# Float32 attention jobs: scores of two heads as row tiles, high parts read from PSUM, moved priorities

## The chip, the cores and the metric

One core of a Trainium2 chip runs the kernel in one launch. The metric is the device time of that launch in microseconds. Names of engines: TensorE (PE in the profile, its weight loads PEld), VectorE (DVE), ScalarE (ACT), GpSimd (POOL); SP issues nearly all DMAs.

## The reference

```python
B, H, S, D = 4, 8, 768, 64
scores = (1 / np.sqrt(D)) * np.matmul(q, k.transpose(0, 1, 3, 2))
keep = (pos[None, :] < n_sink) | ((rel >= 0) & (rel < window))
...
attn = np.matmul(softmax_over_kept_keys, v)
x = attn.transpose(0, 2, 1, 3).reshape(B * S, H * D)
h = np.maximum(x @ moe_w_in, 0.0); y = h * h @ moe_w_out
h = y @ moe2_w_in; out = (h - np.tanh(h)) @ moe2_w_out
```

Four sequences of 768 positions and eight heads of 64 go through attention with 4 sink keys and a window of 128. The result, 3072 rows of 512, goes through two layers with 2048 inner columns: a squared relu, and h - tanh(h). Weights and results are finer than a single rounded product gives: the output must match a float32 (weights: wider) computation.

## The kernel before, in words

**Tiles and stages.** The 3072 rows are eight blocks of 384 (half a sequence each). Attention of a block is eight jobs, one per head (`job`, L294). A job has three query tiles of 128; each meets at most 260 keys and writes one score tile into a PSUM bank. The jobs of blocks 0 and 1 (j < 16, "plain", L452) multiply in float32; the later ones (`scores`, L324, `values`, L412) split q, k and v into a high and a low part of a faster type (float32r) and add products. The layers do the same: every weight half (16 x 2 of each layer) is loaded as 64-bit words (`w_load`, L552), turned into a high and a low part by five or six VectorE or ScalarE instructions (`w_split`, L558), and every product is three matmuls (`mm_a`, L591, line 600; `mm_b`, L605, lines 614 and 616). `step1` (L619) is one of 16 steps of the first layer for a block, `step2` (L651) one of the second for 512 rows.

**A plain job before the change.** q and k lie twice in a tile "raw", on both halves of the 128 partitions (`layout`, L1076), so that a matmul over 128 partitions gives twice the score; the scale of -0.0625 takes that back (L478, L487). For j > 1 each job loads its tile (L305) and its values (L306); the first two are loaded ahead in `prepare` (L832). There are four raw tiles and four value tiles. Then: three score matmuls (L471), for block 0 into two sets of "wide" banks that heads use in turn (`place`, L463), for block 1 into the bank S; a masked copy inside the bank (L475, L482); a minimum with the mask added, written to pcb (`least`, L398, line 403); the exponential (L489); sums, a reciprocal, the scaling (L501, L503); four transposes into the bank T (L512, L513); copies out of it (L271 on ScalarE, L273 on VectorE: the shared `copy`, L265); two triangular selects on POOL (L523, L526). After every second head, `plain_values` (L531) multiplies with the values of two heads, each on its own 64 columns of the array (L539, L544), into the bank O. The result of the pair is copied to px (L548), and `split` (L444) copies px to the high part xh and subtracts to get the low part xl (L449, in the shared `sub`, L276, line 281). xh and xl of all four pairs are the input of the block's 16 steps.

**What sets the order.** `plan` (L699) adds some 6,100 entries with a priority each (lower is earlier; due times worked out from rates per block), what they read and write, and a cost for each engine that could do them (the functions c_act to c_mm, L215 to L250). `Order.solve` (L127) goes through them as a list scheduler and picks for each entry its engine and place; the program is then emitted in that order (L821). Every engine's queue runs in order, SP's loads among them. `run` (L805) takes the tiles and zeroes the sink tiles psk (L814); `switch` (L785) lets tiles of one stage take the room of those of an earlier one.

Of the kernel before, what the change touches and what calls it, by code (L numbers as in the profile page):

```python
# [24 lines left out]
P = 128  # L25
# [34 lines left out]
SQ_S, SQ_B, SQ_D = _fit()  # L60

# [17 lines left out]
class Order:  # L79
# [46 lines left out]

    def solve(self):  # L127
        free = {e: self.AHEAD.get(e, 0.0) for op in self.ops for e in op.engs}
        avail, pend = {e: [] for e in free}, {e: [] for e in free}
# [113 lines left out]
def c_sel(n):  # L243
    return C(0.55 * n + 480, 0.55 * n + 530, True)

# [7 lines left out]
class Fast:  # L253
# [40 lines left out]
    def job(self, j, due):  # L294

        t = self.t
        blk, head = divmod(j, H)
        b, half = divmod(blk, 2)
        plain = j < PLAIN
        nk, nv, k2 = KW[half], NV[half] - 2 * (not plain), j % 2  # L300
        q, r = (j % 4, j % 4) if plain else (k2, j % 3)
        d = due[0]
        if j > 1:
            src, early = self.raw[half][b * H + head], 8 * plain
            self.load(d - 24 - early, [("rq", q), ("rk", q)], lambda: (t["raw", q][:, :QW[half]], src[:, :QW[half]]), P * QW[half] * 4)  # L305
            self.load(d - 23 - early, [("rv", r)], lambda: (t["rv", r][:, :nv * D], src[:, RW[half] - nv * D:]), P * nv * D * 4)  # L306

        def vals():
            return t["rv", r][:, :nv * D].rearrange("p (n d) -> p n d", d=D)
        if plain:  # L310
            self.plain(j, half, head, blk, q, due)
            return
        x = t["raw", q]
        self.copy(d - 16, [("rq", q)], [("qh", k2), ("ql", k2)], lambda: (t["qq", k2], x[:, :N1]), N1)
        self.sub(d - 15, [("rq", q)], [("ql", k2)], lambda: (t["qq", k2][64:], x[64:, :N1], t["qq", k2][64:]), N1)
        self.copy(d - 16, [("rk", q)], [("kh", k2)], lambda: (t["kh", k2][:, :nk], x[:, N1:N1 + nk]), nk)
        self.sub(d - 15, [("rk", q), ("kh", k2)], [("kl", k2)], lambda: (t["kl", k2][:, :nk], x[:, N1:N1 + nk], t["kh", k2][:, :nk]), nk)
# [134 lines left out]
    def plain(self, j, half, head, blk, q, due):  # L452
# [9 lines left out]

        def place(i):  # L463
            return bank["wide", m2, 0] if wide and i == 0 else bank["wide", m2, 1][:, i - 1, :] if wide else bank["S", 0]

        for i in range(3):
            sb = [("wide", m2, i)] if wide else [("S", 0)]
            col, n = self.keys(half, i)

            o.add({"T": c_mm(n, n, slow=1.85)}, due[i] - 14, [("rq", q), ("rk", q)], sb,  # L470
                  lambda e, i=i, col=N1 + col, n=n: nc.tensor.matmul(out=place(i)[:, :n], lhsT=t["raw", q][:, i * P:(i + 1) * P],  # L471
                                                                     rhs=t["raw", q][:, col:col + n], start=True, stop=True))
            if i >= i0 and not wide:
                o.add({"V": c_two(P, True)}, due[i] - 12, sb, sb,
                      lambda e, i=i: nc.vector.copy_predicated(out=place(i)[:, 132:260], mask=self.c["up"][:, 0, :], data=place(i)[:, :128]))  # L475
            if not wide:
                self.least(due[i] - 11, sb, [cbs[i], (*nm, i)], lambda i=i, n=n: place(i)[:, n - 132:n], lambda i=i: t[cb][:, i, :],
                           lambda i=i: t[nm][:, i:i + 1], half, i, -0.0625)  # L478
        if wide:
# [3 lines left out]
        for i in range(3):  # L483
            ks, n = cbs[i:i + 1], self.keys(half, i)[1]
            if wide:
                self.least(due[i] - 11, [("wide", m2, i)], [cbs[i], (*nm, i)], lambda i=i, n=n: place(i)[:, n - 132:n], lambda i=i: t[cb][:, i, :],
                           lambda i=i: t[nm][:, i:i + 1], half, i, -0.0625)  # L487
            o.add({"A": c_sum(132)}, due[i] - 10, ks + [(*nm, i)], ks + [(*ss, i)],
# [42 lines left out]
    def plain_values(self, half, head, blk, j, d):  # L531
        nc, o, t, bank = self.nc, self.o, self.t, self.bank
        ob, x, wins = ("O", 0), ("px", head // 2 % 2), self.windows(half)
        jobs = [(64 * k, (j + k) % 4) for k in range(2)]
# [12 lines left out]
        o.add({"T": C(t_mm, t_mm + 165.0)}, d - 4, [(n, k) for _, k in jobs for n in ("rv", "pps")] + [("ppp", k, i) for _, k in jobs for i in range(3)], [ob], pv)  # L547
        self.copy(d - 3, [ob], [x], lambda: (t[x], bank[ob][:, :N1]), N1, True)  # L548
        self.split(head, blk, d, x, [x])

# [148 lines left out]
    def plan(self):  # L699
# [32 lines left out]
        for q in range(4):  # L732
            if q == 2:
                self.switch(lambda k: k[0][0] == "p" and k[0] not in ("ph", "pt", "pts") or k in (("rq", 2), ("rq", 3), ("rk", 2), ("rk", 3), ("rv", 3)),
                            own, self.x_plain, self.attn)
            for n in range(8):
                self.step1(q % 2, n + 8 * (q // 2), PV[q] + n * PS[q], q // 2)
            if q > 1:
                attention(q)
# [21 lines left out]
        for t in range(NB2):  # L761
            for n in range(NM):
# [7 lines left out]
            ("xe", 1, (6, P), F32R), ("pt", 1, (12, P), F32R), ("pts", 2, (N1,), F32R), ("tmp", 1, (512,), F32), ("x", 1, (N1,), F32))  # L770
    PLAINS = (("raw", (2, 3), (QW[1],), F32), ("rv", (3,), (NV[1] * D,), F32), ("pcb", 4, (3, 132), F32), ("pnm", 4, (3,), F32), ("pss", 4, (3,), F32),
              ("prs", 4, (3,), F32), ("pxe", 2, (3, P), F32), ("ppp", 4, (6, P), F32), ("psk", 2, (96,), F32), ("pps", 4, (P,), F32), ("px", 2, (N1,), F32))
    AFTER = (("x2h", 2, (NE, N2), F32R), ("x2l", 2, (NE, N2), F32R))
# [31 lines left out]
    def run(self):  # L805
        tc, nc = self.tc, self.nc
        with ExitStack() as self.st:
# [5 lines left out]
            for i in range(2):  # L813
                nc.gpsimd.memset(self.t["psk", i], 0.0)  # L814
            pool = self.x_wide.enter_context(tc.tile_pool(name="wide", bufs=1, space=PSUM, reuse_waits="tile"))
            for i in range(2):
# [8 lines left out]
def prepare(tc, cp, ns_wd, f, raw):  # L825
# [6 lines left out]
    for j in range(2):  # L832
        (nc.sync if j else nc.scalar).dma_start(out=f.t["raw", j][:, :QW[0]], in_=raw[0][j, :, :QW[0]])
    for j in range(2):
# [241 lines left out]
def layout(q, k, v, n_sink, window, moe_w_in, moe_w_out, moe2_w_in, moe2_w_out):  # L1076
# [10 lines left out]
    for half, ks, vs_ in ((0, [sk, kb[0], sk, kb[1], sk, kb[2]], range(3)), (1, [kb[2], sk, kb[3], sk, kb[4], sk, kb[5]], range(2, 6))):  # L1087
        qk = np.concatenate([qt[:, :, half * N1:(half + 1) * N1]] + ks, 2)
        vv = np.concatenate(vs + [vb[:, i] for i in vs_], 2)
        res[f"raw{half}"] = np.ascontiguousarray(np.concatenate([np.concatenate([qk, qk], 1), vv], 2))  # L1090
    for n, wi, wo in (("w1", moe_w_in, moe_w_out), ("w2", moe2_w_in, moe2_w_out)):
# [11 lines left out]
```

## Time and profile before

| | |
|---|---|
| Median of 3 runs | 1240.0 us (1239.92 to 1240.06) |
| The profiled execution's own time | 1239.75 us |
| Its span | 1237.7 us |
| PE busy | 1222.7 us |
| DVE busy | 1005.0 us |
| ACT busy | 654.5 us |
| POOL busy | 156.8 us |
| Granted TensorE clock | 0.999 of full speed |
| Loaded and stored | 79.56 MB read, 14.16 MB written |

The span is the time from the first to the last instruction of the program; the execution's own time has some 2 us around it. The sections below use these views: busy time of each engine in chosen stretches, the chain of work that ended last (followed back from the end of the program), who waited for whom, instructions in order of time, and groups of instructions with their durations. Matmuls are pipelined: the time from one matmul's start to the next one's start is what it takes from TensorE, and its own duration is longer.

### The profile page before, as it was taken

What the parts mean: (1) busy time and instruction counts of PE and PEld (TensorE: products, weight loads), DVE (VectorE), ACT (ScalarE), POOL (GpSimd) and SP (SyncE); (2) the same over time, 40 slices, a digit from 0 to 9 for tenths busy, and PEclk for the clock granted to TensorE, in tenths of its full rate; (3) what the DMA queues carried; (4) which work ended last, traced back from release to release, by engine and by line L of the source; (5) the groups of instructions that cost most, each with busy time, mean ns of one, the idle gap of its engine ahead of it and who ended that gap; (6) DMA issues with size and microseconds to landing.
All of it is one profiled execution on the core that took longest, in us unless ns stands there. A gap on an engine that the chain in (4) does not pass through costs nothing.

```text
span 1237.7 us, 18796 instructions
## 1 busy us (share of the span) xinstructions
PE 1222.7 (99%) x6570; PEld 1100.8 (89%) x6570; DVE 1005.0 (81%) x2363; ACT 654.5 (53%) x1625; POOL 156.8 (13%) x194
## 2 busy tenths in 40 slices
PE   8999999999999999999999999999999999999998
PEld 6889999999999999999999988888888888888886
DVE  8999997777777777777679999877877878777775
ACT  7777885655656656656545666433433423323333
POOL 3321331112222112211103000000000000000000
PEclk9999999999999999999999999999999999999999
DMA  8982232212122112221158700200200100000001
GB/s 286 319 310 77 73 92 62 70 50 82 51 63 86 56 52 78 62 88 50 35 175 265 237 30 1 69 1 1 69 1 9 60 1 1 35 1 1 34 1 37
DMA packets 41577, 95.01 MB, mean 77 GB/s; under 512 B 4610, under 2 KB 18434, under 8 KB 41474
## 3 DMA queue, kind: packets, MB, share of 16 engines
q1 hardware_dynamic: 41330, 93.34, 23.4%
q8 instruction: 53, 0.87, 0.3%
q10 hardware_dynamic: 144, 0.40, 0.1%
q14 instruction: 50, 0.41, 0.1%
HBM read 79.56 MB, written 14.16 MB: 76 GB/s over the span
## 4 chain that ended last, share of the span: by engine, by line
PE 88%; DVE 6%; ACT 2%; DMA 1%; issue 1%; POOL 0%; DVEq 0%; POOLq 0%; ACTq 0%; SPq 0%
PE ph L600 24%; PE acc L616 22%; PE acc L614 18%; PE S L600 5%; PE O L600 5%; PE T L600 5%; PE O L426 2%; PE S L338 1%; PE S L337 1%; PE T L371 1%; DVE w L281 1%; DVE wd L584 1%; DMA raw<-yd 1%; PE S L471 1%; PE O L428 1%
## 5 line engine op out<-in xcount | busy, mean ns | idle before, releaser
L600 PE MATMUL ph<-xh,w 128*128 128x384 f32 x1024 | 338.5, 342 | 3.2 <-ACT r L630 2.3
L614 PE MATMUL acc<-gh,w 128*128 128x384 f32 x1024 | 321.3, 338 | 0.2 <-DVE w L281 0.2
L616 PE MATMUL acc<-w,g2h 128*128 128x512 f32 x768 | 296.9, 397 | 0.0
L600 PEld LDWEIGHTS ph<-xh,w 128*128 128x128 f32 x1024 | 191.5, 188 | 7.4 <-ACT r L630 4.1
L614 PEld LDWEIGHTS acc<-gh,w 128*128 128x128 f32 x1024 | 190.5, 188 | 1.3 <-DVE w L281 0.5
L616 PEld LDWEIGHTS acc<-w,g2h 128*128 128x128 f32 x768 | 144.4, 188 | 33.8
L614 PE MATMUL acc<-gl,w 128*128 128x384 f32 x512 | 173.6, 339 | 0.1
L600 PE MATMUL ph<-xl,w 128*128 128x384 f32 x512 | 172.6, 337 | 0.0
L616 PE MATMUL acc<-w,g2l 128*128 128x512 f32 x384 | 151.9, 395 | 0.0
L387 POOL TENSOR_SCALAR_AFFINE_SELECT pt<-xe 128x768 fp32r<-128x768 f32 x96 | 87.8, 938 | 301.3 <-DVE xe L383 301.3
L663 DVE TENSOR_SCALAR mk<-u 128x512 uint8<-128x512 f32 x96 | 40.8, 425 | 71.4 <-ACT u L656 71.4
L614 PEld LDWEIGHTS acc<-gl,w 128*128 128x128 f32 x512 | 96.2, 188 | 2.0 <-DVE gl L281 1.1
L600 PEld LDWEIGHTS ph<-xl,w 128*128 128x128 f32 x512 | 96.4, 188 | 1.2 <-DVE xl L281 0.5
L630 ACT ACTIVATE r<-ph 128x384 f32<-128x384 f32 x102 | 50.0, 490 | 75.2 <-PE ph L600 74.3
L616 PEld LDWEIGHTS acc<-w,g2l 128*128 128x128 f32 x384 | 72.1, 188 | 16.9 <-DVE g2l L281 0.5
L347 ACT ACTIVATE cb<-cb,nm 128x132 f32<-128x132 f32 x144 | 58.1, 404 | 48.1 <-DVE nm L403 47.7
L342 DVE COPY_PREDICATED S<-up,S 128x128 f32<-128x128 uint8 x120 | 34.9, 290 | 51.9 <-PE S L338 51.1
L600 PE MATMUL O<-x2h,w 128*128 128x512 f32 x192 | 75.0, 391 | 0.0
L600 PE MATMUL T<-x2h,w 128*128 128x512 f32 x192 | 75.0, 390 | 0.0
L600 PE MATMUL S<-x2h,w 128*128 128x512 f32 x192 | 74.7, 391 | 0.0
L600 PE MATMUL ph<-x2h,w 128*128 128x512 f32 x192 | 74.6, 390 | 0.0
L669 DVE COPY_PREDICATED r<-mk,w 128x512 f32<-128x512 uint8 x96 | 71.5, 744 | 2.7
(202 smaller groups left out, 2471.4 us busy)
## 6 DMA issues: line engine op xcount, KB each, us to landing
wr<-w SPq DMA_DIRECT2D x64, 512.0 KB, 5.4
raw<-raw SPq DMA_DIRECT2D x32, 454.0 KB, 3.4
raw<-raw SPq DMA_DIRECT2D x31, 390.0 KB, 3.2
yd<-y SPq DMA_DIRECT2D x40, 192.0 KB, 2.5
raw<-yd SPq DMA_DIRECT2D x28, 256.0 KB, 2.9
out<-y SPq DMA_DIRECT2D x20, 256.0 KB, 2.3
raw<-raw SPq DMA_DIRECT2D x24, 160.0 KB, 2.2
raw<-raw SPq DMA_DIRECT2D x24, 128.0 KB, 2.1
```

What stands on the lines that cost most here:

```text
L281: (nc.vector if e == "V" else nc.gpsimd).tensor_tensor(out=out, in0=a, in1=b.bitcast(F32), op=ALU.subtract)
L337: nc.tensor.matmul(out=bank[sb][:, :n], lhsT=lhs, rhs=kh[:, col:col + n], start=True, stop=False)
L342: lambda e: nc.vector.copy_predicated(out=bank[sb][:, 132:260], mask=self.c["up"][:, 0, :], data=bank[sb][:, :128]))
L347: lambda e, i=i: nc.scalar.activation(out=t[cb][:, i, :], in_=t[cb][:, i, :], func=AF.Exp, bias=t[nm][:, i:i + 1], scale=-1.0, accum_out=t ...
L387: lambda e, u=u, s=s, sign=sign, op=op: nc.gpsimd.affine_select(out=t[pt].rearrange("p (n t) q -> p n t q", t=2)[:, 2 * u:, s, :], in_=t[x ...
L426: nc.tensor.matmul(out=oo[:, c:c + cnt * P], lhsT=vv[:, b - 2, :], rhs=pt[:, k + 2 * l:k + 2 * l + 3 * cnt - 2:3, :], start=(n == 0 and l ...
L600: nc.tensor.matmul(out=ph[:, :N], lhsT=w[:, a + c * P:a + (c + 1) * P], rhs=b[:, c, :], start=(c == 0 and k == 0), stop=(c == NE - 1 and k ...
L614: nc.tensor.matmul(out=acc[:, :N1], lhsT=w[:, a + e_ * P:a + (e_ + 1) * P], rhs=g, start=st, stop=sp)
L616: nc.tensor.matmul(out=acc, lhsT=g[:, e_ * P:(e_ + 1) * P], rhs=w[:, a:a + 512], start=st, stop=sp)
L630: nc.scalar.activation(out=r, in_=ph, func=AF.Relu)
L663: lambda e: nc.vector.tensor_scalar(out=T[mk], in0=T[u], scalar1=U_MAX, scalar2=None, op0=ALU.is_lt))
L669: lambda e: nc.vector.copy_predicated(out=T[r], mask=T[mk], data=T[w]))
```

## The change

1. Plain scores of block 0: a pair of heads shares one raw tile, head 0 of the pair on partitions 0 to 63, head 1 on 64 to 127 (`layout` and `prepare` put them there; one load per pair). Only the even head adds score entries; each entry issues two matmuls of 64 partitions, one per head, into the two sets of wide banks.
2. Plain scores of block 1: the pair's q shares a tile in the same way; k goes into four tiles zk, one half of each zeroed once (a memset each in `run`), the other loaded per head. The matmul runs over 128 partitions as before, with zeros against the other head's q.
3. The scale becomes -0.125, since a score is no longer doubled.
4. `plain_values` writes xh straight from the bank O and subtracts with the bank as a source; px and its split go.
5. The planner's cost of a select changes from 0.55 n + 480 to 0.75 n + 250, and a table SHIFT adds to the priorities of 83 entries, by their number. By that number, most are in block 0's attention (its loads, minima, reciprocals, copies) and the first weight halves, then the third block's attention, and the last attention block with the first layer's last two blocks and the first loads of the second layer.

```diff
+SHIFT = {int(k): float(v) for k, v in (w.split(":") for w in """
+32:-252.82 39:-170.67 40:-130.76 41:-129.11 62:-308.18 71:-160.81 76:-106.06 77:-118.01 83:-184.85 96:-74.28 97:-246.08 109:3.54
...
+3801:-2.8 3802:-1.8 4046:5.75 4051:0.8 4056:0.8 4077:3.15 4092:-4.65 4129:4 4178:2.55 4179:1.95 4397:-80.25
+""".split())}
     def solve(self):
+        for r, d in SHIFT.items():
+            self.ops[r].prio += d
 def c_sel(n):
-    return C(0.55 * n + 480, 0.55 * n + 530, True)
+    return C(0.75 * n + 250, 0.75 * n + 300, True)
# job
-        q, r = (j % 4, j % 4) if plain else (k2, j % 3)
+        q, r = (j // 2 % 2, j % 4) if plain else (k2, j % 3)
-            self.load(d - 24 - early, [("rq", q), ("rk", q)], lambda: (t["raw", q][:, :QW[half]], src[:, :QW[half]]), P * QW[half] * 4)
+            if not plain:
+                self.load(d - 24, [("rq", q), ("rk", q)], lambda: (t["raw", q][:, :QW[half]], src[:, :QW[half]]), P * QW[half] * 4)
+            elif not head % 2:
+                w = QW[half] if j < H else N1
+                self.load(d - 24 - early, [("rq", q), ("rk", q)] if j < H else [("rq", q)],
+                          lambda: (t["raw", q][:, :w], src[:, :w]), P * w * 4)
+            if plain and j >= H:
+                rows = slice(64 * (head % 2), 64 * (head % 2) + 64)
+                self.load(d - 23.5 - early, [("zk", r)], lambda: (t["zk", r][rows, :nk], src[:64, N1:N1 + nk]), 64 * nk * 4)
# plain
-            o.add({"T": c_mm(n, n, slow=1.85)}, due[i] - 14, [("rq", q), ("rk", q)], sb,
-                  lambda e, i=i, col=N1 + col, n=n: nc.tensor.matmul(out=place(i)[:, :n], lhsT=t["raw", q][:, i * P:(i + 1) * P],
-                                                                     rhs=t["raw", q][:, col:col + n], start=True, stop=True))
+            if not wide:
+                o.add({"T": c_mm(n, n, slow=1.85)}, due[i] - 14, [("rq", q), ("zk", m4)], sb,
+                      lambda e, i=i, col=col, n=n: nc.tensor.matmul(out=place(i)[:, :n], lhsT=t["raw", q][:, i * P:(i + 1) * P],
+                                                                    rhs=t["zk", m4][:, col:col + n], start=True, stop=True))
+            elif not m2:
+                def qk(e, i=i, col=N1 + col, n=n):
+                    for g in range(2):
+                        rows = slice(64 * g, 64 * g + 64)
+                        nc.tensor.matmul(out=place(i, g)[:, :n], lhsT=t["raw", q][rows, i * P:(i + 1) * P], rhs=t["raw", q][rows, col:col + n],
+                                         start=True, stop=True)
+                c = c_mm(n, n, slow=1.85)[0] + 145.0 * (i != 1)
+                o.add({"T": C(c, c + 165.0)}, d - 14, [("rq", q), ("rk", q)], [("wide", g, i) for g in range(2)], qk)
# plain_values
-        self.copy(d - 3, [ob], [x], lambda: (t[x], bank[ob][:, :N1]), N1, True)
-        self.split(head, blk, d, x, [x])
+        c, b2 = head // 2, blk % 2
+        self.copy(d - 3, [ob], [("xh", b2, c)], lambda: (t["xh", b2][:, c, :], bank[ob][:, :N1]), N1, True)
+        o.add({"V": c_two(N1, True)}, d - 2.5, [ob, ("xh", b2, c)], [("xl", b2, c)],
+              lambda e: nc.vector.tensor_tensor(out=t["xl", b2][:, c, :], in0=bank[ob][:, :N1], in1=t["xh", b2][:, c, :].bitcast(F32), op=ALU.subtract))
# tiles, run, prepare, layout
-    PLAINS = (("raw", (2, 3), (QW[1],), F32), ...
+    PLAINS = (("zk", 4, (KW[1],), F32), ...
+            for i in range(4):
+                nc.gpsimd.memset(self.t["zk", i][64 - 64 * (i % 2):, :][:64], 0.0)
-        (nc.sync if j else nc.scalar).dma_start(out=f.t["raw", j][:, :QW[0]], in_=raw[0][j, :, :QW[0]])
+        rows = slice(64 * j, 64 * j + 64)
+        (nc.sync if j else nc.scalar).dma_start(out=f.t["raw", 0][rows, :QW[0]], in_=raw[0][0, rows, :QW[0]])
-        res[f"raw{half}"] = np.ascontiguousarray(np.concatenate([np.concatenate([qk, qk], 1), vv], 2))
+        two = qk.copy()
+        two[:H] = qk[:H].reshape(H // 2, 2, D, -1)[:, ::-1].reshape(H, D, -1)
+        res[f"raw{half}"] = np.ascontiguousarray(np.concatenate([np.concatenate([qk, two], 1), vv], 2))
```

## Rows read from the trace of the kernel before

**Rows 1.** Busy us of each engine by stretch; after PEclk the DMA share and GB/s:

```profile
8.00:26.00 18.00, 16.08 (x113) 12.10 (x113) 16.65 (x85) 17.50 (x81) 5.85 (x13) 1.00 0.88 311
26.00:37.00 11.00, 9.35 (x75) 7.12 (x76) 10.54 (x34) 7.77 (x26) 3.69 (x7) 1.00 0.89 296
37.00:80.00 43.00, 42.40 (x282) 37.61 (x282) 41.73 (x127) 33.36 (x97) 12.80 (x15) 1.00 0.95 333
80.00:97.00 17.00, 16.16 (x102) 13.67 (x101) 16.63 (x35) 12.42 (x31) 6.84 (x11) 1.00 0.61 228
97.00:630.00 533.00, 532.46 (x3302) 529.35 (x3301) 412.73 (x1199) 334.30 (x956) 111.91 (x131) 1.00 0.22 64
630.00:660.00 30.00, 28.07 (x152) 26.12 (x151) 26.51 (x51) 14.67 (x28) 3.90 (x2) 1.00 0.86 276
```

**Rows 2.** The chain that ended last, 0 to 40 us: start us, us, what:

```profile
10.01 1.17 ACT pcb L489 x6
...
20.23 0.40 ACT xh L271
...
31.63 0.81 DVE w L281
```

**Rows 3.** PE's waits, 0 to 100 us: us in total, times, longest us:

```profile
PE T L512 <- ACT pps L271: 1.7, 3, 0.9
PE S L471 <- DVE pnm L403: 1.5, 2, 1.0
...
PE ph L600 <- ACT r L630: 0.6, 1, 0.6
```

**Rows 4.** PE's waits, 600 to 660 us:

```profile
PE ph L600 <- ACT r L630: 1.8, 2, 0.9
```

**Rows 5.** PE's instructions in order of time: start us, us, what:

```profile
18.72 0.39 PE L471 MATMUL one<-raw 128*128 128x132 f32 x2
...
19.82 0.39 PE L471 MATMUL one<-raw 128*128 128x132 f32 x2
...
22.16 0.38 PE L539 MATMUL O<-ppp,raw 128*64 128x256 f32 x1
22.16 0.38 PE L539 MATMUL O<-ppp,rv 128*64 128x256 f32 x1
...
31.57 0.53 PE L600 MATMUL ph<-xh,w 128*128 128x384 f32 x1
31.94 0.33 PE L600 MATMUL ph<-xl,w 128*128 128x384 f32 x1
32.11 0.34 PE L600 MATMUL ph<-xh,w 128*128 128x384 f32 x1
```

**Rows 6.** Groups of 0 to 100 us: shapes, count, busy us, mean ns, idle:

```profile
L482 DVE COPY_PREDICATED two<-up,two 128x256 f32<-128x256 uint8 x8 | 3.4, 420 | 0.0
```

**Rows 7.** The page's DMA issues: count, KB each, us to landing:

```profile
raw<-raw SPq DMA_DIRECT2D x32, 454.0 KB, 3.4
raw<-raw SPq DMA_DIRECT2D x31, 390.0 KB, 3.2
```

**Rows 8.** Tile px: ns shortest/median/longest, first and last start us, shapes:

```profile
L281 DVE TENSOR_TENSOR xl<-px,xh x8: 547/552/874, 20.7 to 93.4; 128x384 fp32r<-128x384 f32 x8
L271 ACT COPY px<-O x7: 457/472/478, 19.6 to 76.4; 128x384 f32<-128x384 f32 x7
L271 ACT CAST xh<-px x5: 503/511/513, 20.1 to 92.3; 128x384 fp32r<-128x384 f32 x5
L273 DVE CAST xh<-px x3: 348/352/354, 25.3 to 77.4; 128x384 fp32r<-128x384 f32 x3
```

**Rows 9.** Tile xe of the later blocks, in the columns of rows 8:

```profile
L383 DVE TENSOR_TENSOR xe<-T,xe x48: 546/558/560, 121.1 to 618.6; 128x384 fp32r<-128x384 f32 x48
L271 ACT CAST xe<-T x47: 462/480/483, 120.2 to 618.1; 128x384 fp32r<-128x384 f32 x47
```

**Rows 10.** POOL in order of time, 4 to 14 us:

```profile
13.34 0.41 POOL L523 TENSOR_SCALAR_AFFINE_SELECT ppp<-pxe 128x256 f32<-128x256 f32 x1 [8.64 <-ACT pxe L271]
```

More of the change, by code (lines that the diff above doesn't have):

```diff
@@ L461, in plain, with place @@
         tb, ob = ("T", 0), ("O", 0)
-        def place(i):
-            return bank["wide", m2, 0] if wide and i == 0 else bank["wide", m2, 1][:, i - 1, :] if wide else bank["S", 0]
+        def place(i, g=m2):
+            return bank["wide", g, 0] if wide and i == 0 else bank["wide", g, 1][:, i - 1, :] if wide else bank["S", 0]
         for i in range(3):
@@ L477, in plain @@
                 self.least(due[i] - 11, sb, [cbs[i], (*nm, i)], lambda i=i, n=n: place(i)[:, n - 132:n], lambda i=i: t[cb][:, i, :],
-                           lambda i=i: t[nm][:, i:i + 1], half, i, -0.0625)
+                           lambda i=i: t[nm][:, i:i + 1], half, i, -0.125)
         if wide:
@@ L486, in plain @@
                 self.least(due[i] - 11, [("wide", m2, i)], [cbs[i], (*nm, i)], lambda i=i, n=n: place(i)[:, n - 132:n], lambda i=i: t[cb][:, i, :],
-                           lambda i=i: t[nm][:, i:i + 1], half, i, -0.0625)
+                           lambda i=i: t[nm][:, i:i + 1], half, i, -0.125)
             o.add({"A": c_sum(132)}, due[i] - 10, ks + [(*nm, i)], ks + [(*ss, i)],
@@ L532, in plain_values @@
         nc, o, t, bank = self.nc, self.o, self.t, self.bank
-        ob, x, wins = ("O", 0), ("px", head // 2 % 2), self.windows(half)
+        ob, wins = ("O", 0), self.windows(half)
         jobs = [(64 * k, (j + k) % 4) for k in range(2)]
@@ L733, in plan @@
             if q == 2:
-                self.switch(lambda k: k[0][0] == "p" and k[0] not in ("ph", "pt", "pts") or k in (("rq", 2), ("rq", 3), ("rk", 2), ("rk", 3), ("rv", 3)),
+                self.switch(lambda k: k[0][0] == "p" and k[0] not in ("ph", "pt", "pts") or k[0] == "zk" or k == ("rv", 3),
                             own, self.x_plain, self.attn)
@@ L770 @@
             ("xe", 1, (6, P), F32R), ("pt", 1, (12, P), F32R), ("pts", 2, (N1,), F32R), ("tmp", 1, (512,), F32), ("x", 1, (N1,), F32))
-    PLAINS = (("raw", (2, 3), (QW[1],), F32), ("rv", (3,), (NV[1] * D,), F32), ("pcb", 4, (3, 132), F32), ("pnm", 4, (3,), F32), ("pss", 4, (3,), F32),
-              ("prs", 4, (3,), F32), ("pxe", 2, (3, P), F32), ("ppp", 4, (6, P), F32), ("psk", 2, (96,), F32), ("pps", 4, (P,), F32), ("px", 2, (N1,), F32))
+    PLAINS = (("zk", 4, (KW[1],), F32), ("rv", (3,), (NV[1] * D,), F32), ("pcb", 4, (3, 132), F32), ("pnm", 4, (3,), F32), ("pss", 4, (3,), F32),
+              ("prs", 4, (3,), F32), ("pxe", 2, (3, P), F32), ("ppp", 4, (6, P), F32), ("psk", 2, (96,), F32), ("pps", 4, (P,), F32))
     AFTER = (("x2h", 2, (NE, N2), F32R), ("x2l", 2, (NE, N2), F32R))
```

5 rows, old and new, of the table SHIFT are left out of this document.

## The prediction

> **What bounds the kernel now.** I read the table of stretches first. From 97 to 630 us TensorE is busy 532.46 of 533.00 us, and from 37 to 80 us 42.40 of 43.00 [rows 1]: there it is the bound, and only less TensorE work or an earlier start of this dense part can help. Time is lost in three places: before 37 us, between 80 and 97 us (16.16 of 17.00) and between 630 and 660 us (28.07 of 30.00).
>
> The chain of waits says what holds the first place. From 8 to 26 us ScalarE is busy 17.50 of 18.00 us [rows 1], and the chain runs through its exponentials (1.17 us for three with their sums, 0.39 each) and the cast of the first finished pair into xh, 0.40 us at 20.23. From 30 to 37 us it runs through VectorE, mostly weight splitting (0.81 us at 31.63) [rows 2]; VectorE has 10.54 of 11.00 us busy there [rows 1]. The scores of the first block stand nowhere on this chain after the first one; TensorE waits on the two other engines. Its idle time says the same: 1.7 us before transposes until ScalarE copied a bank, 1.5 us before scores until VectorE drained theirs, 0.6 us before the first layer's second step until ScalarE's relu; 3.8 us together [rows 3]. All of it lies before 40 us. In the third place 1.8 us are two waits for the relu, 0.9 us each [rows 4].
>
> **The change part by part.**
>
> *Scores of block 0 as row tiles.* Now one head's three scores take from 18.72 to 19.82 us, 1.10 us; eight heads 8.8 us. If a pair's two row tiles run fully side by side this is 4.4 us. That tiles can overlap is seen where column tiles do: the matmuls of a pair's two heads both start at 22.16 [rows 5]. Against it stands the cost of changing what the array does: the first-layer matmul right after a float32 score holds its slot from 31.57 to 31.94, 0.37 us, the next only to 32.11, 0.17 us, so 0.20 us for that change [rows 5]. One change in and one out for each of four pairs is 1.6 us; around each of the twelve pair scores it is 4.8 us. The bounds are therefore a gain of 4.4 us and a loss of 0.4; I take 4.4 - 1.6 = 2.8 us of TensorE time. On the path I cost it at nothing: ScalarE and VectorE carry that stretch, and TensorE's freed time becomes waiting. If their load fell by as much, part of it would count (second rival).
>
> The Trainium skill, "TensorEngine Tiling (Array Packing)", section "Key Properties", says that changing the tiling mode drains TensorE. The 0.20 us is a change of type and not of tiling, so no row here shows that drain. If it came at every change, the TensorE saving would be the -0.4 end, not 2.8 us. The sum takes nothing from either; it is why the rival that spends this saving gets a smaller chance.
>
> *A wait that is added.* A pair's score now needs the banks of both earlier heads drained, where heads alternated between two sets. Behind it on TensorE's queue stand the transposes and value products of the pair before, and ScalarE waits for those. Until the next exponential that is 1.10 us of scores, two changes (0.40 us) and the masked copy, 0.42 us [rows 5, 6]: 1.9 us, three times in the block, 5.7 us. The cover: when the last bank is drained ScalarE still has most of six exponentials (2.3 us) [rows 2], and copies and weight conversions besides. I take 0 and keep 5.7 as the other end.
>
> *Loads.* The first block's q and k now come in once for a pair: four 390 KB loads fewer. In the second block a pair costs 192 KB of q and two zk loads of 131 KB, where it was two of 454 KB. Together 4 x 390 + 4 x (908 - 454) = 3.4 MB less, about 10 us at the 333 GB/s of 37 to 80 us [rows 1, 7]. TensorE's longest waits of the first 100 us [rows 3] name no transfer, so the path gains nothing; with transfers at 0.88 to 0.95 of their time [rows 1] up to 0.5 us may come of it. On SP's queue a pair of block 0 issues three loads for four, one of block 1 five for four; a zk load waits until its buffer's scores are done, and weight loads stand behind it. Their cover is that no such wait shows now; without it a late weight is a VectorE wait of about the same length.
>
> *High parts from PSUM.* A pair now goes PSUM to px, px to xh, then a subtraction from px. The cast disappears: five times 511 ns on ScalarE, three times 352 ns on VectorE [rows 8], so 2.6 and 1.06 us. The copy that stays writes the rounded type: the attention's later blocks do that in 480 ns against 472 for px, and the subtraction with a PSUM source takes 558 ns against 552 [rows 8, 9]. So the price per pair is as before, minus the cast. POOL can no longer take the subtraction, but all eight were VectorE's already.
>
> *Memsets.* Four half tiles of zk are zeroed on POOL at the start. POOL is idle for 8.64 us before its first select at 13.34 [rows 10], and block 1 needs zk much later: nothing, unless VectorE is slowed beside them by up to the 0.32 us between median and longest subtraction [rows 8].
>
> *Priorities and the costs of selects.* Over eighty planner entries get another priority: most in block 0 and its first weights, over a dozen in the third block's attention, some twenty from the last attention block to the first layer's last steps and the first loads of the second. The shorter select cost reorders POOL's callers everywhere. Every order between 97 and 630 us starts from 0.54 us of idle time, so it can only lose there; I take 0, with 1 us of loss as the end.
>
> **The sum.** First place: the missing cast (0.40 us on the chain) and a new order remove half of 3.8 us, 1.9; the ends are 0 and 3.8, and half is taken because ScalarE stays nearly full. Second place: VectorE has 1.06 us less to do before it and TensorE lost 0.84 there: 0.8. Third place: the relu waits behind other ScalarE work, which the moved priorities re-sort: half of 1.8, 0.9, ends 0 and 1.8. Together 3.6 us. The profiled execution took 1239.75 us; minus 3.6 is 1236.15. The median of the three runs, 1240.0, lies 0.25 us above it, so I forecast 1236.4 us.
>
> **The rivals.**
>
> *Nothing to measure.* ScalarE, busy 17.50 of 18.00 us, still sets the end of the first block, or row tiles run one after the other and the change does not do what it says on TensorE, and one order's gain is another's loss. For it: no score on the chain. Against it: 3.7 us of casts leave just these two engines. What is left is the second place and some of the third, 1.5 us: 1238.5 us.
>
> *Everything is found.* The new order fills the first place wholly (3.8 us), removes the relu waits (1.8) and 0.8 in the second, and half of TensorE's saved 2.8 us counts: 7.8 us, 1232.2 us. For it: VectorE's idle 1.35 us and ScalarE's 0.50 between 8 and 26 us, and ScalarE's 3.23 idle between 26 and 37 [rows 1], are enough to be shared better. Against it: half of that saving must pass two nearly full engines.
>
> *Slower.* The pair's shared banks uncover the boundary between pairs: 1.9 us at each of three boundaries, 5.7, the first place gains nothing and 1.7 stay: 1244.0 us. It decides from about 4 us of ScalarE idle time in the first block's stretch, which has 0.50 now. Against it: six exponentials and weight work lie ready.
>
> **How the numbers follow.** The forecast has 0.44 (about 1233.8 to 1237.5), everything found 0.18, nothing to measure 0.25, slower 0.13. A difference of 0.2%, 2.5 us, is about what a measurement can tell from none. So faster than 1237.5: 0.44 + 0.18 = 0.62; within 2.5 us: 0.25; slower: 0.13. The range runs from 1231.0, below the large gain with its row-tile bound, to 1241.0; it leaves out most of the slower case and the far end of the large one.
>
> **What would show it.** Right: the cast of px gone from the profile; the pair's scores starting together on both row halves; TensorE's waits before transposes and block-1 scores about 2 us together; the dense part starting 1 to 3 us earlier; less than 1 us of relu waits near 630 to 660 us, and TensorE still full between. Wrong: ScalarE or VectorE with holes of over 1 us at each pair boundary in the first 26 us; scores of the two halves one after the other; new waits for a transfer on zk or weights; or a dense part that starts where it did.

## The result and the profile after

The changed kernel takes 1247.25 us (median of 5; 1244.7 to 1249.07) against 1240.0: a ratio of 1.0058, interval 1.0043 to 1.0072, so 7.2 us slower. The profiled execution took 1247.6 us, its span is 1245.8.

Busy time by stretch, in the columns of [rows 1]:

```profile
8.00:26.00 18.00, 15.86 (x116) 11.75 (x117) 16.76 (x88) 16.32 (x74) 6.83 (x12) 0.91 0.85 270
26.00:37.00 11.00, 9.36 (x63) 5.98 (x63) 9.18 (x27) 7.26 (x28) 3.77 (x7) 0.85 0.92 291
37.00:80.00 43.00, 40.76 (x276) 35.84 (x275) 40.91 (x129) 31.97 (x89) 9.30 (x12) 1.00 0.91 307
80.00:97.00 17.00, 17.00 (x115) 16.09 (x115) 16.85 (x40) 12.32 (x29) 6.71 (x10) 1.00 0.47 149
97.00:630.00 533.00, 529.19 (x3260) 521.67 (x3259) 413.77 (x1230) 322.16 (x896) 116.20 (x143) 1.00 0.22 65
630.00:660.00 30.00, 28.65 (x159) 27.31 (x158) 22.10 (x45) 12.48 (x25) 2.73 (x2) 1.00 0.66 211
```

Two things differ in a way the prediction had not looked for. In the first two lines the granted clock is 0.91 and 0.85 of full speed instead of 1.00. And from 97 to 630 us, where [rows 1] have 3302 matmuls, there are 3260 in the same 533 us: 42 fewer, at 533 / 3302 = 0.161 us each 6.8 us of work not done by then. Only 532.46 - 529.19 = 3.3 us of it shows as idle time of TensorE; its weight loads, the next column, are busy 529.35 - 521.67 = 7.7 us less. The first layer's xl matmuls (the products with the low part of the attention's result) say the same: their first starts as early as before, their last 7.6 us late. First the kernel before, then the changed one (shortest/median/longest ns, first and last start):

```profile
L600 PE MATMUL ph<-xl,w x512: 331/337/446, 24.7 to 703.0; 128*128 128x384 f32 x171
```

```profile
L631 PE MATMUL ph<-xl,w x512: 333/336/446, 24.8 to 710.6; 128*128 128x384 f32 x171
```

Who waited for whom, TensorE, 0 to 100 us of the changed kernel (answers to [rows 3]):

```profile
PE one L498 <- DMA raw<-raw: 1.5, 1, 1.5
PE ph L631 <- ACT r L661: 1.4, 2, 0.9
...
PE S L492 <- DVE pnm L424: 1.0, 2, 0.6
PE ph L631 <- ACT xh L284: 0.9, 1, 0.9
PE T L541 <- ACT pps L284: 0.8, 1, 0.8
```

The transposes and block-1 scores wait 1.8 us, where it was 3.2; instead a pair's score waits 1.5 us for its load and the first layer 2.3 us for ScalarE. The chain that ended last, 0 to 40 us, has changed its path (in [rows 2] it runs through ScalarE here):

```profile
9.48 2.10 PE two L498 x7
...
14.92 1.08 PE two L498 x8
...
23.39 0.33 SPq L302
...
23.77 5.86 DMA wr<-w
29.65 0.68 ACT wd L604
```

From 9.5 to 23.4 us it goes mostly through TensorE's scores, transposes and value products, and then through a weight load, which stands on SP's queue behind a load of values that waits until value products end. ScalarE waits 1.1 us for that weight.

TensorE's waits again, those of its weight loads, 97 to 630 us, where before the scores' weights waited 1.0 us for VectorE's minimum:

```profile
PEld S L358 <- DVE nm L424: 4.8, 11, 0.6
PEld ph L631 <- ACT r L661: 2.3, 5, 1.1
PEld acc L645 <- ACT y L284: 1.7, 1, 1.7
```

POOL's groups there show a re-sorted middle: 23 subtractions for vv, where before it did 13, and 5 for kl, where it did 2 (shapes, count, busy us, mean ns):

```profile
L294 POOL TENSOR_TENSOR vv<-raw,vv 128x256 fp32r<-128x256 f32 (+1 forms) x23 | 18.8, 818 | 57.6 <-DVE vv L286 47.5 <-ACT vv L284 10.1
...
L294 POOL TENSOR_TENSOR kl<-raw,kh 128x396 fp32r<-128x396 f32 x5 | 5.2, 1046 | 26.6 <-ACT kh L284 26.6
```

TensorE's instructions in order of time show where the clock fell (start us, us, what):

```profile
9.48 2.10 PE L498 MATMUL two<-raw 64*128 64x260 f32 x7 [0.44 <-DVE pnm L424]
...
12.38 0.90 PE L541 MATMUL T<-idr,pcb 128*128 128x128 f32 x3
...
14.26 0.55 PE L541 MATMUL T<-idr,pcb 128*128 128x128 f32 x3 [0.79 <-ACT pps L284]
14.65 0.27 PE L542 MATMUL T<-idr,psk 128*96 128x128 f32 x1
14.85 1.15 PE L498 MATMUL two<-raw 64*128 64x260 f32 x8
15.83 0.39 PE L498 MATMUL one<-raw 64*128 64x132 f32 x4
16.20 0.52 PE L541 MATMUL T<-idr,pcb 128*128 128x128 f32 x3
```

Three transposes take 0.90 us at 12.38 and 0.55 at 14.26; eight row tiles of 260 columns 1.15 us at 14.85, and seven 2.10 at 9.48. The slow ones run at the lower of TensorE's two levels, 1.2 GHz: the granted clock is 0.50 from 10 to 13 us, and from 33 to 38 us it is low once more.

```profile
10.00:13.00 3.00, 3.00 (x14) 2.52 (x14) 2.52 (x16) 2.55 (x14) 0.00 (x0) 0.50 0.45 170
...
33.00:38.00 5.00, 4.63 (x28) 3.16 (x29) 3.77 (x14) 2.50 (x9) 0.37 (x1) 0.66 0.93 281
```

At the full one the row tiles do overlap: a pair's scores take 16.20 - 14.85 = 1.35 us, one head's took 1.10 [rows 5].

### The profile page after: what moved, and what is told of

It reads as the page before. It is cut to its first block, busy times and chain, and to the rows that moved or that the text cites. A ratio compares the mean times of both kernels' runs of the same rounds, so it can differ in the third digit from the quotient of the medians.

```text
span 1245.8 us, 18754 instructions
## 1 busy us (share of the span) xinstructions
PE 1225.8 (98%) x6570; PEld 1100.2 (88%) x6570; DVE 1008.9 (81%) x2404; ACT 639.5 (51%) x1554; POOL 162.0 (13%) x210
## 2 busy tenths in 40 slices
DMA packets 41082, 91.56 MB, mean 73 GB/s; under 512 B 4627, under 2 KB 18963, under 8 KB 40979
## 4 chain that ended last, share of the span: by engine, by line
PE 83%; DVE 10%; ACT 2%; issue 2%; DMA 2%; POOL 0%; SPq 0%; DVEq 0%; POOLq 0%; ACTq 0%
PE acc L647 22%; PE ph L631 21%; PE acc L645 15%; PE O L631 5%; PE S L631 5%; PE T L631 5%; PE O L447 2%; PE S L358 1%; PE T L392 1%; PE S L359 1%; DVE wd L615 1%; PE O L568 1%; DVE wd L617 1%; DVE w L294 1%; DVE kl L294 1%
## 5 line engine op out<-in xcount | busy, mean ns | idle before, releaser
L631 PE MATMUL ph<-xh,w 128*128 128x384 f32 x1024 | 345.9, 343 | 4.0 <-ACT r L661 2.9
L408 POOL TENSOR_SCALAR_AFFINE_SELECT pt<-xe 128x768 fp32r<-128x768 f32 x96 | 81.2, 869 | 251.7 <-DVE xe L404 245.8
L661 ACT ACTIVATE r<-ph 128x384 f32<-128x384 f32 x125 | 61.2, 490 | 85.0 <-PE ph L631 84.1
L286 DVE CAST gh<-r 128x384 fp32r<-128x384 f32 x81 | 29.6, 366 | 72.1 <-ACT r L667 71.3
L294 DVE TENSOR_TENSOR gl<-r,gh 128x384 fp32r<-128x384 f32 x128 | 71.4, 558 | 5.4 <-ACT gh L284 3.6
```

Of the source, the lines that this page charges most:

```text
L286: nc.vector.tensor_copy(out=out, in_=in_)
L294: (nc.vector if e == "V" else nc.gpsimd).tensor_tensor(out=out, in0=a, in1=b.bitcast(F32), op=ALU.subtract)
L408: lambda e, u=u, s=s, sign=sign, op=op: nc.gpsimd.affine_select(out=t[pt].rearrange("p (n t) q -> p n t q", t=2)[:, 2 * u:, s, :], in_=t[x ...
L631: nc.tensor.matmul(out=ph[:, :N], lhsT=w[:, a + c * P:a + (c + 1) * P], rhs=b[:, c, :], start=(c == 0 and k == 0), stop=(c == NE - 1 and k ...
L661: nc.scalar.activation(out=r, in_=ph, func=AF.Relu)
```

## Experiments

Where an order is "fixed", the planner's search gives way to a table that has an engine and a place for each entry; nothing else changes. "Entries" are the planner's. Ratios are to runs of the kernel before on the same chip (medians 1240.3 to 1240.5 us).

### The planner's two settings

Without SHIFT (first), with the old select cost (second), with both undone (third), each on the changed kernel; and the new cost alone on the kernel before (fourth):

```diff
-        for r, d in SHIFT.items():
-            self.ops[r].prio += d
# second
-    return C(0.75 * n + 250, 0.75 * n + 300, True)
+    return C(0.55 * n + 480, 0.55 * n + 530, True)
# fourth, on the kernel before
-    return C(0.55 * n + 480, 0.55 * n + 530, True)
+    return C(0.75 * n + 250, 0.75 * n + 300, True)
```

> The change without the 83 moved priorities; the new cost of a select stays. Theory A, if the priorities carry the loss: 97 to 630 us full again, 1241 to 1243 us. Theory A, if the cost of a select carries it: still 3 us or more of idle TensorE there and 1246 us or more. Theory B: a clock below 0.95 before 40 us, 1245 us or more, whatever the later stretch does.

> The change with the old cost of a select and with the moved priorities, which were given for another order. Theory A, if the cost of a select carries the loss: POOL has fewer subtractions between 150 and 620 us (33 in the changed kernel, 15 before), and TensorE is full there: 1241 to 1244 us. If the priorities carry it: 1246 us or more. Theory B: a clock below 0.95 before 40 us again.

> The change without its planner part: no moved priorities and the old cost of a select; row tiles, zk, and high parts from PSUM stay. Theory A (the planner's inputs spoil the order of the work behind the first 97 us, where the changed kernel has TensorE busy 529.19 of 533.00 us against 532.46 before, and waits of TensorE's loads for VectorE's minimum of 4.8 us against 1.0): the stretch from 97 to 630 us is full again (over 532 us busy) and the time is about 1241 to 1243 us. Theory B (the row tiles leave TensorE too little to do in the first 40 us, its granted clock falls and all that follows is late): the clock falls below 0.95 in some stretch before 40 us as it did (0.91 and 0.85), and the time stays at 1245 us or above.

> The kernel before with the new cost of a select and nothing else: no row tile, no moved priority. If that cost alone spoils the middle: POOL gets more subtractions after 150 us, TensorE is busy 528 to 531 of 533 us from 97 to 630, and the time is 1243 to 1248 us. If it does so only together with the rest of the change: within 2 us of 1240. The clock should stay at 1.00 in either case.

Without SHIFT 1257.05 us (1.0133, interval 1.0108 to 1.0157); old cost 1252.75 (1.0101, 1.0084 to 1.0117); both undone 1250.06 (1.0079, 1.0062 to 1.0096). The new cost alone makes the kernel before some 12.8 us slower: 1253.37 (1.0101, 1.0084 to 1.0117), at full clock from 8 to 26 us, with 3236 matmuls from 97 to 630 us:

```profile
8.00:26.00 18.00, 16.64 (x118) 12.95 (x118) 17.37 (x86) 17.22 (x80) 7.57 (x14) 1.00 0.86 296
...
97.00:630.00 533.00, 528.86 (x3236) 520.56 (x3237) 416.27 (x1227) 319.89 (x895) 116.64 (x139) 0.99 0.22 64
```

So a planner's cost alone can move this kernel by 1%. Where the runs lose their time differs. From 134 to 630 us the kernel before has 3086 matmuls and the changed one 3039. With the old cost of a select it is 3080 (SHIFT kept) and 3084 (both undone), with the new one 3052 (without SHIFT) and 3048 (on the kernel before). So the loss in the middle goes with the new cost, with SHIFT or without it, with the new structure or without it. The two runs with the old cost lose most of their time before 134 us: TensorE is busy 33.2 and 33.6 of the 37 us from 97 to 134, and the granted clock from 8 to 26 us is 0.81 and 0.62. A reason that would fit, not tested: in the trace of the kernel before the selects of 768 and 512 columns take 957 and 879 ns on average, and the old cost gives 902 and 762 for them, the new one only 826 and 634.

SHIFT wins 9.8 us beside the new cost (1257.05 - 1247.25), but not in the middle; with the old cost it loses instead (1252.75 against 1250.06). The two belong together, and neither is the structure's price.

### The clock

Each row-tile matmul issued twice (the second overwrites the same result); the second pair's load issued ahead on ScalarE's queue, which takes the 1.5 us wait for it away; and, on the kernel before, block 0's scores over the first 64 partitions alone, which hold q and k once, one head after the other:

```diff
# first
-                    for g in range(2):
+                    for g in (0, 1, 0, 1):
# second
+    nc.scalar.dma_start(out=f.t["raw", 1][:, :QW[0]], in_=raw[0][2, :, :QW[0]])
# third, on the kernel before (and -0.125 for -0.0625)
-    lhsT=t["raw", q][:, i * P:(i + 1) * P], rhs=t["raw", q][:, col:col + n]
+    lhsT=t["raw", q][:64 if wide else P, i * P:(i + 1) * P], rhs=t["raw", q][:64 if wide else P, col:col + n]
```

> The changed kernel in the same order, with each row tile's score matmul of block 0 issued twice over the same bank (48 more matmuls of 64 partitions, the same result). About 2.8 to 4.4 us more TensorE work in the first 26 us. Theory B (TensorE too idle there, so the clock falls): the clock stays at 1.00 through 8 to 40 us, and the time falls by 2 to 4 us, to 1243 to 1245 us, although there is more work. Theory A, or the clock not bound to that work: the clock falls as before, and the time is the same 1247 us or up to 3 us more.

> The changed kernel in the same order, with the second pair's q and k loaded ahead of everything on ScalarE's queue and not on SP's where the planner put it. TensorE waits 1.5 us for that load now (before the change no score waited for a load). If that wait is what lets the clock fall at 10 us: the clock is 1.00 in 8 to 26 us, and the time falls by 1 to 4 us. If the fall comes from the row tiles themselves: the wait goes, the clock falls there all the same, and the time changes by less than 1.5 us.

> The kernel before in its own order, with block 0's scores taken over the first 64 partitions alone (scale -0.125, the result is the same) and still one head after the other: as many matmuls, as many columns, half the rows at work. If the clock falls because fewer rows of the array work: it falls below 0.95 before 40 us here too, and the time rises by 1 to 8 us. If it falls because the pair's tiles finish in half the time and TensorE then waits: the clock stays at 1.00 and the time within 1 us of 1240.

With twice the work the time is 1245.8 us (1.0044, 1.0028 to 1.0061) at a mean clock of 0.999 to 1.0 in all executions: 1.5 us less in the median, though the intervals overlap. The changed kernel's own scatter follows its clock: 1244.7 at 0.998, 1246.38 to 1247.6 at 0.996, 1249.07 at 0.995. The late load of the second pair does not decide it: without that wait the time is 1247.8 us (1.0046, 1.0029 to 1.0064), and from 8 to 26 us the granted clock is 0.72. But the pause stays in that run, since TensorE now waits 1.7 us at the same place for VectorE's minimum. That such a pause alone does not bring the clock down is shown by other runs: with the repeat TensorE waits 1.6 us there, and the clock holds.

Half the rows alone cost the kernel before 6.7 us: 1247.02 us (1.0054, 1.0041 to 1.0068). Same instructions, columns and order; TensorE's instructions in order of time:

```profile
14.00 0.90 PE L512 MATMUL T<-idr,pcb 128*128 128x128 f32 x3
...
19.16 1.94 PE L471 MATMUL two<-raw 64*128 64x260 f32 x4
21.03 0.90 PE L512 MATMUL T<-idr,pcb 128*128 128x128 f32 x3
...
22.07 2.22 PE L539 MATMUL O<-ppp,raw 128*64 128x256 f32 x12
24.13 0.82 PE L544 MATMUL O<-pps,raw 96*64 96x128 f32 x12
24.88 0.55 PE L512 MATMUL T<-idr,pcb 128*128 128x128 f32 x3
```

Everything takes nearly twice as long up to 24 us, the unchanged transposes over 128 rows too (0.90 against 0.55), and TensorE is busy 18.00 of 18.00 us from 8 to 26; the clock rises only during the value products over 128 partitions. The clock column missed it, which is why durations are read beside it:

```profile
8.00:26.00 18.00, 18.00 (x71) 12.54 (x71) 11.14 (x59) 11.87 (x55) 3.47 (x7) 1.00 0.60 201
```

So TensorE can stay at 1.2 GHz without any pause. In the changed kernel, though, two row tiles work side by side on both halves of the rows; that its clock falls for the same reason is not shown.

### The structure in the old order

Fixed to the order of the kernel before: only the high parts straight from PSUM; the whole changed structure; the same with row tiles issued twice:

```diff
# Order.solve
+        fixed = [(w[0], int(w[1:])) for w in zlib.decompress(base64.b85decode(FIXED)).decode().split(",")]
...
+                heapq.heappush(heap, (fixed[op.rank][1], op.rank, op))
```

> The kernel before, with every instruction kept at its place and on its engine as its planner had put it, and one part of the change alone: the high parts are written straight from the bank and the low parts subtracted from it; px and its eight casts are gone. By the prediction's step (one cast of 0.40 us on the chain, 1.06 us less VectorE work ahead of the second stall) it is 0.4 to 1.9 us faster than the kernel before. Rival: everything else keeps its place, so the time saved turns into waits for the next thing, and it is within 0.5 us of it.

> The whole structure of the change (row tiles, paired loads, zk, high parts from the bank), with no select cost and no moved priority at work: every instruction that both kernels have stands in the order and on the engine that the kernel before gave it, and the new ones stand where the ones that they replace stood, moved back only as far as what they need forces it. Theory C (what the change lost came from the planner's new order; the structure is good or harmless): 1235 to 1241.5 us. Theory B (the structure itself costs: the pair's banks are waited for and the clock falls): 1243 to 1250 us, with a granted clock below 0.95 in a stretch before 40 us.

> The same, with each row tile's score matmul issued twice. Theory B with the clock as its means: the clock stays at 1.00 and the time falls by 1 us or more below the kernel of e10. If the clock does not fall in e10 in the first place: no gain, or up to 2 us more for the added matmuls.

High parts alone: 1239.77 us (0.9997, 0.9988 to 1.0006), at most 1.5 us of gain and not told from none. The structure: 1245.37 (1.0042, 1.0028 to 1.0056), half speed from 10 to 23 us; with the repeat 1244.24 (1.0032, 1.002 to 1.0044) at full clock. So with the clock held 3.9 us remain (1244.24 against 1240.3). First the structure, then with the repeat:

```profile
8.00:26.00 18.00, 15.88 (x78) 9.90 (x79) 12.24 (x66) 13.21 (x57) 3.79 (x9) 0.62 0.45 141
```

```profile
8.00:26.00 18.00, 14.39 (x116) 10.03 (x116) 13.01 (x68) 13.74 (x59) 3.86 (x9) 1.00 0.52 157
```

All three engines have holes now. ScalarE's instructions of the run with the repeat show four of its, and TensorE's waits from 0 to 40 us stand below them:

```profile
12.02 0.41 ACT L584 ACTIVATE pcb<-pcb,pnm 128x132 f32<-128x132 f32 x1 [0.85 <-DVE pnm L490]
...
13.94 0.40 ACT L584 ACTIVATE pcb<-pcb,pnm 128x132 f32<-128x132 f32 x1 [1.08 <-DVE pnm L490]
...
17.34 0.41 ACT L584 ACTIVATE pcb<-pcb,pnm 128x132 f32<-128x132 f32 x1 [0.97 <-DVE pnm L490]
...
19.13 0.27 ACT L350 COPY ppp<-T 128x128 f32<-128x128 f32 x1 [0.71 <-PE T L608]
```

```profile
PE two L564 <- DVE pnm L490: 1.2, 4, 0.4
...
PE one L564 <- DVE pnm L490: 1.0, 2, 0.7
```

The exponentials wait for minima, which wait for the pair's scores, which wait 2.2 us in all until minima have drained the banks. That is the mechanism of the slower rival, and the 3.9 us lie between the 0 and the 5.7 us that the prediction gave this wait; the paired loads and zk are in this run too and were not taken out one by one.

### The select's cost, split

The new cost up to 384 columns only (the selects of blocks 0 and 1 have at most 384, the later ones 512 or more), without and with the repeat; then the first of these with the 34 moved priorities of rank 861 and up left out:

```diff
-    return C(0.75 * n + 250, 0.75 * n + 300, True)
+    return C(0.75 * n + 250, 0.75 * n + 300, True) if n <= 384 else C(0.55 * n + 480, 0.55 * n + 530, True)
# third, besides
-            self.ops[r].prio += d
+            self.ops[r].prio += d if r < 860 else 0.0
```

> The changed kernel with the new cost of a select kept for the plain jobs (128 x 384 and less) and the old one for the later blocks' selects (512 and 768 columns). TensorE's order is the same as in the changed kernel up to about 120 us, so the first 97 us should be as they were, the falls of the clock among them. If the cost of a select spoils the middle (theory A in the form that e1 and e2 left: with the old cost the distance to the kernel before stood still from 104 us on, with the new one it grew by 5 us), TensorE is busy over 531.5 of the 533 us from 97 to 630 and the time falls by 4 to 7 us, to 1240 to 1243 us. If the middle's loss comes from the moved priorities or from what stays late of the first part, it stays within 2 us of 1247.

> The same with each row tile's score matmul issued twice, which held the clock at 1.00 in e4 and made 1245.8 us of 1247.25. If the fall of the clock and the middle's order are two separate losses, they add: 1 to 3 us below the kernel with the split cost alone, 1238 to 1241 us. If the one hid the other, the time is that of the split cost alone, within 0.7 us.

> The changed kernel with the new cost of the select only up to 384 columns, and of the 83 moved priorities only those of rank below 860 (the rest, 35 of them from rank 861 on, left out). The run with the split cost alone took 1245.85 us and lost 4.6 us between 134 and 220 us. If the moved priorities from rank 861 on make that loss: 1240.5 to 1243 us. If the first part's order or the structure makes it: 1245 to 1249 us, with the loss at the same place.

1245.85 us (1.0043, 1.0026 to 1.006), 1245.33 (1.0035, 1.0022 to 1.0047), 1242.37 (1.0015, 1.0006 to 1.0025). The split alone helps the time little, and the repeat adds nothing that the intervals tell from none. But behind 220 us the loss is mostly gone: from 220 to 630 us there are 2541 matmuls, where the changed kernel has 2521 and the kernel before 2552; from 134 to 220 us there are 517, where those have 520 and 536. Without the late priorities another 3.5 us come back, with 521 and 2552 matmuls in the two stretches. Beside the old cost of the long selects these only hurt; what they do beside the new one was not run by itself.

### Whose are the 7 us of the middle?

Fixed orders again, on the changed structure. Hybrid: the first 764 of the changed kernel's 6101 entries (those its planner starts before its own 112 us) in the changed order, the 5337 later ones in the old order. Then with the repeat; then the mirror, early old and late changed:

```diff
# the table of places; k_new, k_old: an entry's place in either order
+        place = k_new if start_new < 112000 else 10000 + k_old   # hybrid
+        place = k_old if start_new < 112000 else 10000 + k_new   # mirror
```

The engines go with the places: 307 of the later entries stand on another engine in the changed order than in the old one.

> The changed kernel's code; of its planner's 6120 entries the first 764 (those that its planner starts before its own 112 us) keep the changed order, all later entries stand in the order of the kernel before. Theory (the later order alone loses the 8 us between 114 and 611 us): 1239 to 1242 us, even with the kernel before at 114 us and even from there to the end. Rival (the first part leaves something behind, buffers or data that come late, whose price falls due later whatever the order): 1245 to 1248 us, with a loss of 4 us or more after 114 us.

> The same order as the run before it, with each of block 0's row-tile scores' matmuls issued twice. Theory (the row tiles' half-speed stretches cost 1 to 1.5 us in the changed order, the later order 8 us, and the two add): 1238 to 1240.5 us, at or a little below the kernel before. Rival (what the repeat gained in the changed kernel was order, not clock): the same as the run before it or 0.5 us more.

> The mirror of the first run of this set: the first 764 entries in the order of the kernel before, all later entries in the changed order. Theory: the loss of the fixed early order, 4.3 to 5.8 us, and the 8 us of the later order add: 1251 to 1254 us. Rival (the later loss belongs to the changed first part): 1244 to 1247 us, no loss after 114 us.

Hybrid 1240.84 us (1.0003, 0.9994 to 1.0013), with the repeat 1240.11 (0.9995, 0.9986 to 1.0005), mirror 1252.62 (1.0092, 1.0075 to 1.0109). The middle of the hybrid, then of the mirror:

```profile
97.00:630.00 533.00, 532.44 (x3303) 529.73 (x3302) 412.77 (x1196) 334.73 (x956) 111.91 (x130) 1.00 0.22 64
```

```profile
97.00:630.00 533.00, 529.13 (x3248) 519.81 (x3247) 416.85 (x1235) 323.02 (x899) 117.72 (x145) 1.00 0.23 66
```

3303 matmuls against 3248, with the same code. The later order (places and engines) costs 1247.25 - 1240.84 = 6.4 us behind the changed early part and 1252.62 - 1245.37 = 7.3 us behind the old one: the loss is its own and not left behind by the first part. The hybrid's executions also scatter with their clock: 1238.42 and 1238.44 us at 0.998, 1240.7 to 1242.6 at 0.993 to 0.995. The profiled one has the changed kernel's first fall, from 8 to 26 us at 0.91, but from 26 to 37 us the full clock and 76 matmuls against 63, in the same order. So there is something to win. In the median the repeat wins 0.7 us of it here.

### Holding the clock for less

The hybrid with the repeat for the first two pairs only, and with the repeat of the 132-column tile only:

```diff
-                    for g in range(2):
+                    for g in ((0, 1, 0, 1) if head < 4 else (0, 1)):
# second
+                    for g in ((0, 1, 0, 1) if i == 0 else (0, 1)):
```

> The hybrid (changed early order, old later order) with the row-tile scores' matmuls issued twice for the first two pairs of block 0 only. If the repeats of the first pairs alone keep the full clock through block 0: 1238.3 to 1239.8 us, where the hybrid's fastest executions lie (1238.4 at a mean clock of 0.998), below the kernel before. If the clock falls at the later pairs instead: 1240.5 to 1242 us with a mean clock of 0.993 to 0.996 as in the hybrid.

> The hybrid with only the first query tile's score (132 columns) issued twice, in all four pairs: a third of the repeat's added columns or less. If the clock needs the whole repeat: 1240.5 to 1242 us at a mean clock of 0.993 to 0.996. If the short repeat is enough: 1238.3 to 1239.8 us at 0.998 or more.

1238.97 us (0.9985, 0.9976 to 0.9994) and 1238.19 (0.998, 0.9971 to 0.9989), at 0.997 to 1.0 and 0.998 to 0.999 in every execution. The second is the fastest version found, 2.3 us below the kernel before, and clear of the hybrid (0.9994 to 1.0013). In its trace TensorE still waits 2.0 us before the second pair's scores, and the clock holds. Its lines, by stretch and of the xl matmuls:

```profile
8.00:26.00 18.00, 15.70 (x131) 11.89 (x132) 17.52 (x90) 17.06 (x78) 7.42 (x14) 1.00 0.87 282
...
97.00:630.00 533.00, 532.67 (x3305) 530.06 (x3304) 412.84 (x1195) 334.07 (x954) 112.04 (x130) 1.00 0.22 64
```

```profile
L697 PE MATMUL ph<-xl,w x512: 333/336/446, 23.9 to 700.7; 128*128 128x384 f32 x171
```

## Why the prediction was wrong

The sign was wrong, and 1247.25 us lies above the whole range. Two steps failed.

**Priorities and the costs of selects.** The step for the stretch from 97 to 630 us, "I take 0, with 1 us of loss as the end", rested on a true sentence, that the order can only lose there, and then bounded the loss by nothing. The later order costs 6.4 us, nearly the whole result, and the runs put the loss in the middle down to the new cost of a select. The row that should have warned was there: 0.54 us of idle time in 533 says that thousands of matmuls stand in an order with no slack, and an edit that re-sorts POOL's callers "everywhere" undoes it. A view that shows no waste prices a reshuffle from one side only.

**Row tiles, "On the path I cost it at nothing".** Their overlap was sized about right: four pairs at 1.35 us against 8.8 save 3.4 us of TensorE time at the full clock, where 2.8 was taken, and the change in and out, 0.40 us a pair there, is at most 1.35 - 1.10 = 0.25. What the step left out is the clock, which no sentence weighed although its column stands in [rows 1]. TensorE fell to 1.2 GHz, and the scores that it slowed came onto the path (2.10 us of the chain at 9.48). Against the execution and the variant that hold the clock this cost 1.5 us (the repeat, not clear of noise by itself) to 2.5 us (the execution at 0.998) here, 2.6 us in the hybrid (1240.84 against 1238.19, clear of it), and 6.7 us in the kernel before with half the rows alone.

**The added wait** was costed at 0 with 5.7 us as its other end. In the old order it shows, 3.9 us with the clock held; ScalarE idles 18.00 - 13.74 = 4.3 us, where the rival put the turning point at about 4. In the changed order it is covered: the hybrid, with the same shared banks, is level with the kernel before. So the rival's mechanism exists, and its 1244.0 us came nearest, but by luck: it is not what makes the changed kernel slow.

**Loads** were costed at nothing, and a sign of being wrong came: a score waits 1.5 us for its pair's load, and a weight load of 5.86 us stands on the chain. Neither makes the kernel slow: without the first the time is the same (another wait takes its place), and the hybrid, level with the kernel before, has such a weight load on its chain as well (4.93 us at 23.77). Of the 3.4 MB less, 95.01 MB became 91.56.

**High parts:** the casts are gone, and the copy (477 ns) and the subtraction (550 ns) cost what the prediction took. The gain on the time is not told from none, where 0.4 us of the first place's 1.9 had been put down to it.

**The three places.** First: 1.4 of 3.2 us of its two main waits went, near the forecast half, but 1.5 us for a load came in and the first layer's waits for ScalarE rose from 0.6 to 2.3. Second: TensorE is busy 17.00 of 17.00, the 0.8 us came, but not for the reason given: with the casts alone gone it is 15.96, and it is full with the changed early order (17.00 in the hybrid), so this term came right by luck. Third: the relu waits fell from 1.8 us [rows 4] to 0.5, while a wait of 0.8 us for a copy on VectorE came in. With the old later order and the clock held, the fastest version ends 2.3 us below the kernel before, where 3.6 were forecast.

Beside this result a rule of the Trainium skill, "TensorEngine Tiling (Array Packing)", section "Theoretical Speedup", which gives up to twofold where a dimension is at most 64: by the rows above it is 2 x 1.10 / 1.35 = 1.6 on the scores themselves, and the kernel's time shows none of it as long as the clock falls (the hybrid's 1240.84 us against 1240.54).

What stays open: why the clock falls in the changed kernel, and why the repeat of the short tile holds it as well as that of all. The loss of 6 to 7 us in the middle is shown for the later order as a whole, and goes with the new cost of a select; which entries make it is not shown, and POOL's added subtractions and the late minima are only the visible ones.

## What to carry over

Before halving TensorE's work in a stretch where other engines set the pace, read the granted clock and the durations of unchanged matmuls there: less work there can go with a lower clock, and what follows in the stretch is slowed too. An edit of a planner's cost or priority is a change of every order behind it, and where the engine has no idle time its price is open upward; test it by itself, and test a change of structure with the old order frozen. When an early part is re-tuned, keep the later order fixed.

## What was not expected of the hardware

Issuing the same row-tile matmul twice made a kernel faster: in the hybrid 1238.19 us against 1240.84, with the short tiles alone repeated. With all of them repeated four kernels gained 0.5 to 1.5 us each, none clear of noise by itself. TensorE busy 18.00 of 18.00 us can be an engine at half speed with the clock column at 1.00; three transposes at 0.90 us instead of 0.55 gave it away. And the hybrid scatters by 4 us (1238.42 to 1242.62), its times rising as its mean clock goes from 0.998 to 0.993; the kernel before scatters as much beside it (1238.52 to 1243.01, at 0.999 and 0.997). Where the clock fell in executions that were not profiled is not shown.
